# Order of the first planned steps, products of zeros on TensorE, and the planned length of u's load and product in an attention and feed-forward kernel

## The chip, the cores and the metric

The kernel runs on one core of a Trainium2 chip. The metric is the device time of one execution in microseconds (us). Eight runs of the kernel before gave 187.0, 188.34, 188.75, 187.57, 188.7, 187.79, 188.61 and 188.26 us: median 188.3 us.

The core has a matrix engine (TensorE, in the profile PE; PEld is its loading of the stationary operand), a vector engine (VectorE, DVE), an engine for activation functions (ScalarE, ACT), a general engine (GpSimd, POOL) and a queue (SyncE, SP) that issues nearly all transfers between main memory and the core's own memory. Each takes its instructions strictly in the order in which the program gives them. They wait for one another by semaphores.

## The reference

An attention with a decaying state (4 sequences, 8 heads, 768 steps, 48 numbers per head), and behind it a feed-forward layer without a gate:

```python
for t in range(S):
    kt, vt, rt, wt = (k[:, :, t].copy(), v[:, :, t].copy(), r[:, :, t].copy(), w[:, :, t].copy())
    cur = np.einsum('bhd,bhe->bhde', u[None] * kt, vt)
    y[:, :, t] = np.einsum('bhd,bhde->bhe', rt, state + cur)
    state = wt[:, :, :, None] * state + np.einsum('bhd,bhe->bhde', kt, vt)
...
x = np.ascontiguousarray(attn_out.transpose(0, 2, 1, 3)).reshape(B * S, H * D)   # 3072 x 384
h = x @ w_in                    # 384 x 2048
g = np.maximum(0.01 * h, h)
return (g @ w_out).astype(np.float32)    # 2048 x 384
```

## The kernel before

The 3072 rows are cut into 24 chunks of 128 rows, 6 per sequence. Every chunk goes through two parts.

The attention part (the scan): logarithm of w (L360, ACT), running sums of it by products with triangular matrices (L544 and L554, or L714 and L719, PE), exponentials of the sums (L370, ACT), products of r and k with them into a tile called rk (L300, DVE or POOL), transposes of rk (L418, PE, copied out at L295 or L297 into rkT), scores (L652 or L764, PE), a mask (L436, DVE), the products that make y in the bank yp (L669 and L677, or L794 and L799, PE), the sum with the bonus term of u (L467, DVE), and the transpose of y (L481, PE) whose copy is xT. The state is carried from chunk to chunk (products at L617 or L775, sums at L456). The first four chunks are done as two pairs by `pair` (64 rows of each of two interleaved halves), all others by `single`.

The feed-forward part: for each chunk four groups of 12 products xT by w_in (L837, "up", one group for each quarter of the 2048 columns, 512 columns of a bank hp), a leaky ReLU (L879, ACT) into g, and four groups of 4 products g by w_out (L898, "down", in the bank op). The chunk's result is copied to o and sent out (L915).

All inputs are 32-bit, and the weights are cast to 16 bits on the core (L295 on ACT, L297 on DVE and POOL) in halves: w_in comes in four loads (quarters 0 to 3, L319), w_out in four (L324), each of 768 KB. Tile in4 holds quarter 0 of w_in, in5 quarter 1, in6 quarter 2, in7 quarter 3; in8, in9, in10 and in0 hold the quarters of w_out. Before them the pairs' w, k, r and v are loaded (L493, 384 KB each).

Nothing is issued in the order of the source. Each operation is a `step` of a `Plan`, with an engine, a planned duration, its dependencies and a priority. `Plan.order` plays the steps through once, at build time: whenever an engine is free it takes the ready step with the smallest priority, and the order of the planned starts is the order in which the instructions are written into the engines' queues. So the planned durations and priorities decide the order alone; the chip does not know them. `EARLY` is a list of step numbers found by a search: a step in it gets a priority ahead of all others, by its place, and a letter behind the number gives the engine (a = ACT, v = DVE, p = POOL).

While TensorE has no step in the first 24 us of the plan (`WARM`), the last loop of the kernel writes products of a tile of zeros into the bank op1 (L933): as many as fit into the planned gap ahead of each PE step, at an assumed length each. `spread_u` (L495 to L507) loads u on ACT's queue, spreads it over the 128 partitions by a 32-bit product on PE (L504) and copies it to ub (L507).

Of the kernel before, what the change touches and what calls it, by code (L numbers as in the profile page):

```python
# [126 lines left out]
def kernel(  # L127
# [32 lines left out]
    CASTS = 21  # L160

    EARLY = """
        0 4 1 2 3 5 8 61 7 6 12 58 11 16 13 14 15 21 32 59 17 23 24 18 20p 19 22 28 9a 60 29 30 10a 33
        25 26 31v 40 27 117 64 34 65a 51 36 41a 44 52 63 114 46 42 126 62 45 35 67 66 120 43 71 123 37
        53 47 129 68 132 48 69 135 72 38 75p 49 70 76 74 77p 78 50 81 79 73 87v 54 82 39 118a 85 80 96v
        83 119p 138 86 55 84a 91 115 116 56 95 88v 57 713 128p 715 89 714 97 717 716 127p 98v 719 718 99
        140 122p 729 90v 720 100 121 730 102 723 124a 125p 101 721 724 92v 103 722 727 93 130a 170 104
        94 725 728 131v 105 107 726 106v 731 108 133a 737 109 733 738 134v 110 734 747 136 137p 139 745
        111 748 141 735 142 112 746 144 154v 261 732 113 736 145 172 174 752 147 749 159 149p 155v 171
        146 739 753 148 742 750 200 156 158 152 143a 157v 150 160 755 229 153 151 176 743 162 161 177  # L170
        186 231 756 763 165 265 764 164 230 191 178 758 187v 740 765 232 179 163 759 751 181p 180 202
        233 166 188 766 204 167 190 182 173 245 184 767 206 168 185v 183a 754 192 169v 768 193 741 207
        769 246 194 209 201 771 208 234v 757 770 247 216 262 772 760 210
    """
    blocks = [1] * NCH

# [53 lines left out]
    with tc.manual_schedule():  # L230
# [50 lines left out]
        plan = Plan()  # L281

        def step(eng, dur, fn, pri, reads=(), writes=(), deps=(), wire=None, rows=0, **alts):

            d = list(deps)
            for x in writes:
                d += x.old
            i = plan.add(eng, dur, fn, d, pri, wire, rows, {eng: dur, **alts} if alts else None)
            for x in (*reads, *writes):
                x.steps.append(i)  # L290
            return i
# [204 lines left out]
        def spread_u():  # L496
            u_row = step(
                "ACT", 0.5,
                lambda: nc.scalar.dma_start(out=ur[:], in_=u.rearrange("h d -> (h d)").unsqueeze(0)),
                -1, wire=0.05)  # L500
            up = pre_r.take()
            s_ub = step(
                "PE", 0.7,
                lambda: nc.tensor.matmul(up.t[:, 0:DM], lhsT=onef[:], rhs=ur[:], start=True, stop=True),  # L504
                -1, writes=[up], deps=[u_row])
            return step(
                "ACT", 0.5, lambda: nc.scalar.copy(out=ub[:], in_=up.t[:, 0:DM]), 0.05, reads=[up], deps=[s_ub])  # L507
# [6 lines left out]
        def pair(n):  # L514
# [19 lines left out]
            if n == 0:  # L534
                u_ld = spread_u()
# [155 lines left out]
        def single(n):  # L691
# [12 lines left out]
            if n == 0:  # L704
                u_ld = spread_u()
# [216 lines left out]
        for rank, word in enumerate(EARLY.split()):  # L922
            i = int(word.rstrip("avp"))
# [5 lines left out]
        at = 0.8  # L929
        for i in plan.order():  # L930
            if plan.eng[i] == "PE" and at < WARM:
                for _ in range(int((plan.start[i] - at) * 0.7 / 0.13)):
                    nc.tensor.matmul(  # L933
                        op_r.tiles[1][:, 0:256], lhsT=zeros[:, 0:128], rhs=zeros[:], start=True, stop=True)
                at = plan.start[i] + plan.dur[i]
            if plan.alts[i]:
                plan.fn[i](plan.eng[i])
            else:
                plan.fn[i]()
# [30 lines left out]
```

## Time and profile before

| | before |
|---|---|
| median of 8 runs | 188.3 us |
| the profiled execution | 187.0 us |
| its span, from first to last instruction | 185.3 us |
| PE busy | 177.3 us (96%) |
| DVE, ACT, POOL busy | 65%, 63%, 55% |
| products of zeros (L933) | 60, busy 10.5 us |
| products up (L837) | 1152, busy 78.0 us |
| products down (L898) | 384, busy 75.2 us |

Columns of a line of the page's part 5: line, engine, operation, output <- input with their shapes, count | busy us, mean ns of one | idle time of the engine just before, and what ended it. A row of the timeline gives the start, the length (until the end of the last of the merged instructions), and the same names; an idle time over 0.15 us stands in brackets with its releaser. The ends of products are modelled, since they are pipelined: what a group of products occupies is read from start to start. Such differences are used below: 0.65 us for 4 products down, 0.67 us for 12 products up.

The landing times of the loads that matter here, read from the releasers and the transfer records of the profiled execution: the pairs' eight loads at 4.5, 6.0, 7.5, 9.0, 10.5, 12.0, 13.5 and 14.9 us, the eight loads of weights at about 18.2, 20.2, 22.6, 24.5, 26.5, 28.6, 30.7 and 32.9 us.

### The profile page before, as it was taken

The page shows a single profiled execution, that of the slowest core. Times are in us where ns is not written, and L with a number is a line of the kernel's source. Part 1 is how long each engine was busy: PE and PEld are TensorE (multiplying, and loading weights), DVE is VectorE, ACT ScalarE, POOL GpSimd, SP SyncE. Part 2 cuts the span into 40 slices and gives each one's busy share as a digit, 9 for nine tenths or more (in the row PEclk, how much of TensorE's full clock was granted, in tenths as well). Part 3 has the DMA queues.
Part 4 walks back from the last instruction along what each step waited for, and adds up shares of the span by engine and source line. Part 5 has one row for each costly group of instructions (what it writes and reads, how often), then busy time and mean ns, then how long its engine had stood idle before and what let it go on. Part 6 is the DMA issues. An engine that isn't in the chain of part 4 may idle for free.

```text
span 185.3 us, 6316 instructions
## 1 busy us (share of the span) xinstructions
PE 177.3 (96%) x2608; PEld 139.3 (75%) x2608; DVE 120.5 (65%) x232; ACT 116.0 (63%) x254; POOL 101.1 (55%) x142
## 2 busy tenths in 40 slices
PE   7989889999999999999999999999999999999992
PEld 4658767877788788887877787778878778788671
DVE  2388776658777787987668786667656676725111
ACT  3776847589665797688677578645465564633330
POOL 7798571143875798878784474361874445620000
PEclk9999999999999999999999999999999999999999
DMA  6999999889599989897999797976999999581202
GB/s 150 261 262 370 382 377 324 165 175 211 135 233 199 187 169 207 176 203 158 161 229 170 153 209 144 201 172 151 219 132 216 159 233 131 128 126 42 67 0 85
DMA packets 116383, 34.62 MB, mean 187 GB/s; under 512 B 109697, under 2 KB 114818, under 8 KB 116354
## 3 DMA queue, kind: packets, MB, share of 16 engines
q1 hardware_dynamic: 116352, 34.22, 86.0%
q8 instruction: 20, 0.33, 0.8%
q14 instruction: 9, 0.07, 0.1%
q10 hardware_dynamic: 2, 0.00, 0.0%
HBM read 25.17 MB, written 4.72 MB: 161 GB/s over the span
## 4 chain that ended last, share of the span: by engine, by line
PE 81%; DMA 8%; SPq 6%; issue 1%; POOL 1%; DVE 1%
PE op L898 33%; PE hp L837 33%; DMA in<-in_moe_w_out_dram 5%; SPq L493 5%; PE se L764 3%; PE yp L799 2%; DMA xT<-y 2%; PE cp L714 2%; PE yp L775 2%; PE yp L794 1%; POOL w_out_b L297 1%; SPq L319 1%; PE so L418 1%; PE se L418 1%; PE yp L481 1%
## 5 line engine op out<-in xcount | busy, mean ns | idle before, releaser
L879 ACT ACTIVATE g<-hp 128x512 bf16<-128x512 f32 x96 | 57.2, 597 | 40.0 <-PE hp L837 38.3
L837 PE MATMUL hp<-xT,w_in_b 128*128 128x128 bf16 x1152 | 78.0, 219 | 0.6 <-DMA xT<-y 0.3
L898 PE MATMUL op<-w_out_b,g 128*128 128x384 bf16 x384 | 75.2, 326 | 0.9 <-POOL w_out_b L297 0.9
L837 PEld LDWEIGHTS <-w_in_b 128*128 128x128 bf16 x1152 | 68.4, 98 | 7.3 <-DMA xT<-y 0.7
L898 PEld LDWEIGHTS <-g 128*128 128x128 bf16 x384 | 33.5, 98 | 16.8 <-issue 1.0
L300 POOL TENSOR_TENSOR sb<-s,a 128x384 bf16<-128x384 f32 x17 | 14.4, 845 | 29.9 <-DVE s L456 14.3
L300 POOL TENSOR_TENSOR ru<-in,ub 128x384 f32<-128x384 f32 x22 | 22.6, 1028 | 7.7 <-DMA in<-in_r_dram 7.7
L300 POOL TENSOR_TENSOR vs<-in,dg 128x384 f32<-128x384 f32 x22 | 18.9, 859 | 8.4 <-DVE dg L393 8.1
L300 POOL TENSOR_TENSOR ru<-ru,in 128x384 f32<-128x384 f32 x20 | 20.8, 1041 | 0.9
L436 DVE TENSOR_TENSOR m<-se,maskb 128x512 bf16<-128x512 f32 x20 | 13.8, 688 | 11.2 <-PE so L764 8.0
L467 DVE TENSOR_TENSOR y<-yp,vs 128x384 bf16<-128x384 f32 x24 | 13.3, 554 | 10.2 <-PE yp L799 7.4
L300 DVE TENSOR_TENSOR rk<-in,ek 128x384 bf16<-128x384 f32 x18 | 13.5, 752 | 3.7 <-ACT ek L370 2.5
L370 ACT ACTIVATE cp<-cp 128x384 f32<-128x384 f32 x22 | 10.6, 482 | 6.3 <-DVE ci L729 6.3
L393 DVE TENSOR_REDUCE dg<-ru 128x8 f32<-128x384 f32 x24 | 13.1, 545 | 2.0 <-POOL ru L300 1.9
L360 ACT ACTIVATE lw<-in 128x384 bf16<-128x384 f32 x24 | 12.2, 520 | 3.5 <-DMA in<-in_w_dram 3.1
L729 DVE TENSOR_TENSOR ci<-cp,lw 128x384 f32<-128x384 f32 x20 | 11.0, 551 | 5.0 <-PE cp L719 3.3
L300 DVE TENSOR_TENSOR rk<-in,cp 128x384 bf16<-128x384 f32 x22 | 12.0, 547 | 2.5 <-ACT cp L370 1.9
L436 DVE TENSOR_TENSOR m<-so,maskb 128x512 bf16<-128x512 f32 x20 | 13.6, 680 | 0.0
L297 DVE COPY o<-op 128x384 f32<-128x384 f32 x10 | 5.6, 557 | 11.1 <-PE op L898 11.0
L933 PE MATMUL op<-zeros 128*128 128x256 bf16 x60 | 10.5, 303 | 1.1 <-DVE zeros L268 1.1
L370 ACT ACTIVATE ek<-ci 128x384 f32<-128x384 f32 x20 | 10.4, 519 | 0.8 <-POOL ru L300 0.7
L297 POOL CAST vb<-in 128x384 bf16<-128x384 f32 x19 | 10.2, 539 | 0.6 <-DMA in<-in_v_dram 0.6
(117 smaller groups left out, 210.9 us busy)
## 6 DMA issues: line engine op xcount, KB each, us to landing
out_dram<-o SPq DMA_DIRECT2D x24, 192.0 KB, 3.1
in<-in_w_dram SPq DMA_DIRECT2D x20, 192.0 KB, 4.1
in<-in_r_dram SPq DMA_DIRECT2D x20, 192.0 KB, 3.7
in<-in_k_dram SPq DMA_DIRECT2D x20, 192.0 KB, 3.7
in<-in_v_dram SPq DMA_DIRECT2D x20, 192.0 KB, 3.6
in<-in_moe_w_in_dram SPq DMA_DIRECT2D x4, 768.0 KB, 11.4
in<-in_moe_w_out_dram SPq DMA_DIRECT2D x4, 768.0 KB, 12.8
in<-in_w_dram SPq DMA_DIRECT2D x2, 384.0 KB, 4.9
```

The lines of the kernel that those rows point to most:

```text
L297: (nc.vector if e == "DVE" else nc.gpsimd).tensor_copy(out=o, in_=i)
L300: (nc.vector if e == "DVE" else nc.gpsimd).tensor_tensor(out=o, in0=a, in1=b, op=ALU.mult)
L360: lambda: nc.scalar.activation(out=lw.t[:, :, 0:D], in_=wn.t, func=AF.Ln),
L370: "ACT", 0.5, lambda: nc.scalar.activation(out=out.t[:], in_=i, func=AF.Exp, scale=scale),
L393: lambda: nc.vector.tensor_reduce(out=dg.t[:], in_=ru.t[:], axis=AX.X, op=ALU.add),
L436: lambda par=par: nc.vector.tensor_tensor(out=m.t[:, par], in0=gt(sc[par].t), in1=mask.unsqueeze(1).to_broadcast([128, NP, 128]), op=ALU.m ...
L467: lambda: nc.vector.tensor_tensor(out=y.t[:], in0=hd(yp.t[:, 0:DM]), in1=vs.t[:], op=ALU.add),
L729: lambda: nc.vector.tensor_tensor(out=ci.t[:], in0=hd(cp.t[:, 0:DM]), in1=lw.t[:, :, 0:D], op=ALU.add),
L837: nc.tensor.matmul(hp.t[:, a * N : (a + 1) * N], lhsT=w_in_b[:, t, (j + a) * 128 : (j + a + 1) * 128], rhs=xT[:, t, c0 : c0 + N], start=(a ...
L879: lambda hp=hp, g=g, j=j, J=J, N=N: nc.scalar.activation(out=g.t[:, j : j + J, 0:N], in_=hp.t[:, 0 : J * N].rearrange("p (a n) -> p a n", ...
L898: nc.tensor.matmul(op.t[:, 0:DM], lhsT=g.t[:, j, off : off + 128], rhs=w_out_b[:, j, :], start=(j == 0), stop=(j == NJ - 1))
L933: nc.tensor.matmul(op_r.tiles[1][:, 0:256], lhsT=zeros[:, 0:128], rhs=zeros[:], start=True, stop=True)
```

## The change

Three numbers in the code and the list `EARLY`. The list, cut to its first two lines:

```diff
     EARLY = """
-        0 4 1 2 3 5 8 61 7 6 12 58 11 16 13 14 15 21 32 59 17 23 24 18 20p 19 22 28 9a 60 29 30 10a 33
-        25 26 31v 40 27 117 64 34 65a 51 36 41a 44 52 63 114 46 42 126 62 45 35 67 66 120 43 71 123 37
...
+        0 4 1 2 3 5 8 58 7 6 11 60 12 14 13 16 20p 17 21 59 15 32 26 22 24 18 19 23 27 30 61 33 10v 25a
+        28 9v 29a 36 34 40 63 117 31v 62 35 41 44 66 45 42 114 67 120 51 68 71 87 126 43 69 123 76 72
...
@@ spread_u
                 lambda: nc.scalar.dma_start(out=ur[:], in_=u.rearrange("h d -> (h d)").unsqueeze(0)),
-                -1, wire=0.05)
+                -1, wire=0.75)
             up = pre_r.take()
             s_ub = step(
-                "PE", 0.7,
+                "PE", 1.6 / 1.8,
                 lambda: nc.tensor.matmul(up.t[:, 0:DM], lhsT=onef[:], rhs=ur[:], start=True, stop=True),
@@ the last loop
-                for _ in range(int((plan.start[i] - at) * 0.7 / 0.13)):
+                for _ in range(int((plan.start[i] - at) / 0.22)):
                     nc.tensor.matmul(
                         op_r.tiles[1][:, 0:256], lhsT=zeros[:, 0:128], rhs=zeros[:], start=True, stop=True)
-                at = plan.start[i] + plan.dur[i]
+                at = plan.start[i] + plan.dur[i] * (1.8 if plan.start[i] < 6 else 1)
```

The old list has 272 entries, the new one 339. `Plan.order` multiplies a planned PE duration by 1.8 when it starts before 6 us; the last loop now does the same when it counts the gap.

The steps and their dependencies are the same in both kernels; 34 steps of the first chunks change their engine. What the two built programs hold, read from their instruction streams:

Products of zeros: 60 before, 48 after. Ahead of u's product 12 and 13; between u's product and the first running sums 10 and 4 (and 1 before, none after, among the sums); ahead of the first transposes 6 and 5; the rest in ones to sevens up to the first product up.

The loads on SP, in order (pair 2 is chunks 2 and 3):

```
before: pair 0 w k r v | pair 2 v w k r | w_in 1, 0 | w_out 0 | w_in 2, 3       | w_out 1, 2, 3
after:  pair 0 w k r v | pair 2 w r k v | w_in 1, 0 | w_in 2  | w_out 0 | w_in 3 | w_out 1, 2, 3
```

Behind these the single chunks' loads (192 KB each) also change places among themselves.

PE, from the products that make y of chunk 0 on (z = products of zeros; up q c0 = group of 12 products up, quarter q, chunk 0):

```
before: y0 z5 turn-y0 z5 turns y1 turn z1 turn z6 turn-y1 state z1 | up0 c0, up0 c1, z1, up1 c0, up1 c1,
        down0 c0, scores, down0 c1, up2 c1, up2 c0, y2, up3 c1, up3 c0, turn-y2, scores, down1 c0, ...
after:  y0 z1 turns z3 turn-y0 z4 y1 state z2 turn-y1 z1 | up0 c0, up0 c1, z1, up1 c0, up1 c1,
        scores, up2 c0, up2 c1, down0 c0, down0 c1, y2, up3 c0, up3 c1, turn-y2, scores, down1 c1, ...
```

Here y0 is L669 with L677 of chunk 0, turn-y the transposes at L481, state the 16 products at L617 of pair 2, scores L652, y2 the products of chunk 2.

ACT, from about 16 us on:

```
before: xT0, pa, copy rkT, w_in 1 (half), copy rkT, copy rkT, w_in 0 (half), xT1, leaky ReLUs ...
after:  copy rkT, vb, copy rkT, pa, vb, w_in 1 (half), xT0, w_in 1 (other half), w_in 0 (half), xT1, leaky ReLUs ...
```

The other half of w_in 0 goes from DVE to POOL, one half of w_in 1 from POOL to ACT; the halves of w_out 0 are both on POOL before, one on DVE and one on POOL after; of w_out 1 one on ACT and one on DVE before, one on ACT and one on POOL after; of w_out 2 one on ACT in both, the other from DVE to POOL; of w_out 3 one on DVE and one on POOL before, both on DVE after. The shrunken states of pair 2 (L300, sb<-s,pa) go from DVE to POOL.

More of the change, by code (lines that the diff above doesn't have):

```diff
@@ L162 @@
     EARLY = """
-        0 4 1 2 3 5 8 61 7 6 12 58 11 16 13 14 15 21 32 59 17 23 24 18 20p 19 22 28 9a 60 29 30 10a 33
-        25 26 31v 40 27 117 64 34 65a 51 36 41a 44 52 63 114 46 42 126 62 45 35 67 66 120 43 71 123 37
-        53 47 129 68 132 48 69 135 72 38 75p 49 70 76 74 77p 78 50 81 79 73 87v 54 82 39 118a 85 80 96v
-        83 119p 138 86 55 84a 91 115 116 56 95 88v 57 713 128p 715 89 714 97 717 716 127p 98v 719 718 99
-        140 122p 729 90v 720 100 121 730 102 723 124a 125p 101 721 724 92v 103 722 727 93 130a 170 104
@@ L168 @@
[L168 to L172, printed above, removed]
@@ L173 @@
-        769 246 194 209 201 771 208 234v 757 770 247 216 262 772 760 210
+        0 4 1 2 3 5 8 58 7 6 11 60 12 14 13 16 20p 17 21 59 15 32 26 22 24 18 19 23 27 30 61 33 10v 25a
+        28 9v 29a 36 34 40 63 117 31v 62 35 41 44 66 45 42 114 67 120 51 68 71 87 126 43 69 123 76 72
+        75p 129 73 46 79 70 80a 77p 52 132 81 47 65a 78 37 82 53 83 74 85 64a 48 96 135 118a 86v 49 38
+        50 84 39 119 54 91v 95 115p 116 138 55 97 56 713 57 92v 98 715 93 714 122p 121 717 716 99 94 719
+        718 88v 100 127p 141 720 721 128v 723 722 101 729 724 102 730 125p 124a 89 103 90v 725 104 727
@@ new lines @@
+        130p 131 172 105 107 726 106v 732 108 728 733 109 133a 134p 737 734 731 738 735 136 139 747 110
+        137v 748 140 745 142 111 739 170 143v 746 144 112 740 736 145 171 186 113 742 147 751 158 229
+        149 146 752 743 159 148 154 231 152 162 753 749 160v 155 174 741 758 165 200 750 150 153v 176
+        759 187 201 755 156 151a 177 763 157 202 233 188 161 191 764 179 163 230 245 178 754 164 190 756
+        757 181p 192v 166 173 204 765 180 184 167 206 744 182 185 766 207 262 183 168 208 760 216 261
@@ L174 @@
+        169v 767 193 210 209 771 217 768 194 761 235 769 772 195 211p 762 175a 212 218 232 775 770 189
+        236 196 213 776 214 203 246 773 197 237 779 215 239 263 198 774 247 220 264 782 265 222 199 785
+        223 238 241 248 293 777 249 234v 250 240 267 780 778 205 294 242 219 243 221 268 781 783 295 224
+        244 277 786 784 296 225 251 252 787 226 788
     """
```

## The prediction

> **What bounds the kernel now.** First the page's parts 1 and 4 (busy times, and the chain of work that ended last):
>
> ```profile
> PE 177.3 (96%) x2608; PEld 139.3 (75%) x2608; DVE 120.5 (65%) x232; ACT 116.0 (63%) x254; POOL 101.1 (55%) x142
> PE 81%; DMA 8%; SPq 6%; issue 1%; POOL 1%; DVE 1%
> ```
>
> TensorE is 81% of the chain; the transfers and their queue, 14%, can only be at the start. So second the chain in order of time, around the place where it goes over to PE:
>
> ```profile
> 11.70 0.74 SPq L319
> 12.49 10.10 DMA in<-in_moe_w_out_dram
> 22.64 2.28 POOL w_out_b L297 x2
> 24.96 0.81 PE op L898 x4
> ```
>
> Up to 22.6 us a load of w_out sets the pace, then its two casts one behind the other on POOL, and from 24.96 us PE never waits long. Third, what PE waited for in the first 45 us, and its timeline there:
>
> ```profile
> PE op L898 <- POOL w_out_b L297: 0.9, 1, 0.9
> PE op L544 <- ACT lw L360: 0.7, 1, 0.7
> PE se L652 <- issue: 0.3, 1, 0.3
> PE hp L837 <- DVE w_in_b L297: 0.3, 1, 0.3
> ```
>
> ```profile
> 21.05 1.51 PE L837 MATMUL hp<-xT,w_in_b 128*128 128x128 bf16 x24 [0.28 <-DVE w_in_b L297]
> 22.40 0.27 PE L933 MATMUL op<-zeros 128*128 128x256 bf16 x1
> 22.58 1.50 PE L837 MATMUL hp<-xT,w_in_b 128*128 128x128 bf16 x24
> 24.96 0.81 PE L898 MATMUL op<-w_out_b,g 128*128 128x384 bf16 x4 [0.89 <-POOL w_out_b L297]
> 26.08 0.82 PE L898 MATMUL op<-w_out_b,g 128*128 128x384 bf16 x4
> 26.74 1.50 PE L837 MATMUL hp<-xT,w_in_b 128*128 128x128 bf16 x24
> 28.18 0.36 PE L669 MATMUL yp<-sb,rkT 128*64 128x96 bf16 x8
> ```
>
> After 25 us PE loses 0.34 us at 31 us and 0.35 us near the end, where the last chunk's xT lands; all else is products that both kernels hold. So the change is worth what it takes out of PE's time up to its dense stretch: I compare the moment at which PE starts y2 (L669 of chunk 2, 28.18 us before), because both kernels have by then done the same products: up quarters 0 to 2 and down quarter 0 for two chunks, one group of scores.
>
> **What stands between 21.05 and 28.18 before.** Six groups up at 0.67 (two take 1.34 in the chain), two down at 0.65, scores 0.38 (25.70 to 26.08): 4.02 + 1.30 + 0.38 = 5.70 us. The other 1.4 us of 7.13 are 0.19 at 22.4 (a zero, and the wait for bank hp), 1.04 from 23.92 (22.58 + 1.34) to 24.96 (the wait for POOL's casts of w_out), 0.09 and 0.10 of seams.
>
> **The change, first up product.** In the new ACT queue the copy xT0 stands behind the cast of w_in quarter 1, which cannot start before its load has landed:
>
> ```profile
> 16.34 0.48 ACT L295 COPY xT<-yp 128x384 bf16<-128x384 bf16 x1
> 18.19 0.83 ACT L295 CAST w_in_b<-in 128x768 bf16<-128x768 f32 x1 [0.36 <-DMA in<-in_moe_w_in_dram]
> 20.22 0.83 ACT L295 CAST w_in_b<-in 128x768 bf16<-128x768 f32 x1 [0.23 <-DMA in<-in_moe_w_in_dram]
> ```
>
> Behind xT0 waits bank yp, for it y1 on PE, and behind y1 all of PE. Step by step: cast from 18.19; the next ACT instruction starts 0.1 before its end (18.93, as the trace has it), xT0 takes 0.48 to 19.41; y1 at 19.47 with 0.91 (y2 took 28.18 to 29.09), to 20.38; the sum y1 on DVE starts 0.18 later (as 29.09 to 29.27 did) and takes 0.56, to 21.12; the transposes at 21.18 with 0.17; one zero 0.11; first up product at 21.46. State products (0.45) and two zeros lie under the DVE sum. The other condition: w_in 0 lands at 20.2, its half on POOL takes between 0.83 and 1.15 us (POOL's casts of w_in), DVE's took 0.77: 21.1 to 21.4. So the start is 21.46 against 21.05, 0.4 later. Bounds: 21.1, if only the fastest cast counted, and 21.9, if POOL's half took as long as DVE's two casts at 32.94 together (1.67 us, from 20.2).
>
> **The change, behind it.** The third load of weights is now w_in 2, and the groups up2 stand ahead of down0. So: 21.46 + 5.70 + 0.19 for hp + 0.2 for seams = 27.55 for y2, against 28.18: 0.63 earlier. That is the 1.04 no longer waited, less the 0.41 of the later start. It holds if nothing else is late; landing (by its place among the loads), longest cast, and need:
> - scores at 24.3: DVE's last state sum stands behind the cast of w_in 2 (landing 22.6, 0.98 at most) and takes 0.56: 24.2. The tightest.
> - up2 at 24.7: DVE 23.6, POOL behind one sb (0.83 from 21.65) 23.8.
> - down0 at 26.1: 24.5, POOL 1.19: 25.7; DVE's half beside it.
> - up3 at 28.5: 26.5, on ACT behind the leaky ReLU of up2: 27.7.
> - down1 at 30.3: 28.6 + 1.19 = 29.8. Down2 and down3 at 33 and 36: 31.9 and, two casts by DVE in turn at 32.94 with 1.67, 34.6.
> A late hand-over costs what it is late: 0.1 to 0.4 us each. Later order, singles' loads included: PE did not wait over 0.15 us from 31 to 168 us before; I take nothing, bounds 0.3 either way (its waits of 0.28 and 0.34 are the nearest rows).
>
> **Edits I cost at nothing.** Zeros ahead of u: 13 at 0.213 from 1.12 end at 3.89, u's product takes 0.85 (3.79 to 4.64), four zeros at 0.109, 5.18; then the sums wait for the second logarithm (5.44), while before ten zeros held them to 5.74. So the scan starts 0.25 us earlier. Hidden behind the landing of w_in 1 at 18.2; without that cover it would be the same 0.25 gained. v of pair 2 lands 4.4 us later (14.9 for 10.5), w 1.5 earlier (10.5 for 12.0): v is needed by the state products at 20.4, covered by the wait for xT0.
>
> The pause of 0.34 at 31 us lies inside scores (start to start 0.53 lost) and no releaser is shown. The same scores follow the same groups in the new order, so I keep it; bounds: 0.53 gained, or 0.53 lost once more.
>
> **Sum.** 187.0 - 0.6 = 186.4 us on the profiled execution. That one is the fastest of the eight, 1.3 below the median; the 0.6 is taken off the median: 188.3 - 0.6 = 187.7 us. What a measurement can tell from no change is some 0.5%, 0.9 us.
>
> **Rivals.**
>
> *The array goes slow in the longer idle time (the slower side).* What the zeros do is seen in these rows:
>
> ```profile
> 1.12 2.74 PE L933 MATMUL op<-zeros 128*128 128x256 bf16 x12 [1.12 <-DVE zeros L268]
> 4.64 1.27 PE L933 MATMUL op<-zeros 128*128 128x256 bf16 x10
> ```
>
> and in the busy times of the stretch from 1 to 4 us (by engine; then granted clock, DMA share, GB/s):
>
> ```profile
> 1.00:4.00 3.00, 2.88 (x13) 1.85 (x14) 1.16 (x13) 1.08 (x1) 2.41 (x12) 1.00 0.70 171
> ```
>
> The same product comes every 0.213 us at first and every 0.109 us (1.10 for ten) from 4.64 on, after 3.5 us of work, though the granted clock (1.00) shows nothing. Before, PE then never idles over 0.73 us. In the new order turn-y0 (15.82 before) has up to four groups of transposes (0.22) and some zeros more ahead, so about 16 to 17.3; with its 0.17 and four zeros PE is empty from 16.6 to 17.9, until y1 at 19.47: 1.6 to 2.9 us idle. If that makes it slow again, the next 3.5 us of work take up to twice as long: 1.75 to 3.5 us, on the path. Then 188.3 - 0.6 + 1.75 to 3.5 = 189.4 to 191.2, say 190. It decides from 1.5 us of loss on. Against it: 0.73 of idle cost nothing; no row shows 2 us.
> [...]
>
> *The gain is eaten.* Scores 0.1 to 0.3 late, down0 0.2 late, a second pause of 0.3: 0.6 gone. The margins of 0.1 to 0.5 speak for it, that they are taken with the longest casts against. 188.1 to 188.6, say 188.3; this is also what comes out if the new order does not remove the wait.
>
> *More than forecast.* The pause falls elsewhere (0.53 gained), or y1 comes 0.35 sooner: 188.3 - 0.6 - 0.5 = 187.2, at best 186.9.
>
> **Numbers.** Forecast 0.45, more 0.20, eaten 0.18, slow array 0.17. Faster by over 0.5% (below 187.4): all of "more" and 0.2 of the forecast's 0.45, whose own range is 187.3 to 188.1 with the medians' scatter of a few tenths: 0.40. Slower (above 189.2): the slow array and 0.03 of the eaten: 0.20. Same: 0.40. Range: 186.6 (more, with scatter of 0.3) to 189.5 (the near end of the slow array).
>
> **What would show it.** In the new profile: first L837 near 21.4 and not 21.05; no wait of L898 for w_out near 25; y2 of chunk 2 near 27.5; an idle time of about 2 us before y1, released by the ACT copy of xT; products of y1 and up at 0.67 a group, not 1.3, and 48 products of zeros. Wrong it is if up groups behind that idle time take over 1 us, if L652 or L898 between 24 and 36 us wait for DVE or POOL, or if waits over 0.3 us appear on PE after 36 us.

## The result, and the profile after

| | before | after |
|---|---|---|
| median | 188.31 us (59 runs, 186.3 to 189.29) | 189.29 us (22 runs, 187.71 to 189.74) |
| profiled execution, its span | 187.0, 185.3 us | 189.97, 188.3 us |
| first product up (L837, now L840) | 21.05 us | 21.89 us |
| y2 (L669, now L672) | 28.18 us | 29.08 us |

The ratio is 1.0047, 95% interval 1.003 to 1.0065: slower by half a per cent, where 0.3% faster was forecast. (The ratios in this text leave out runs more than 1.5% above the fastest of their kernel; among the experiments below that is five of twelve in a_oldzeros and three of twelve in a_pause and in a_oz66, so there the ratio lies below that of the medians.) All lines of the new source stand three further down. The new page, parts 1 and 4:

```profile
PE 178.6 (95%) x2596; PEld 138.8 (74%) x2596; DVE 122.0 (65%) x230; ACT 116.7 (62%) x254; POOL 105.4 (56%) x144
PE 85%; DMA 5%; ACT 3%; issue 2%; DVE 2%; SPq 0%; DVEq 0%; ACTq 0%
```

The shares of transfers and of SP's queue have fallen from 14% to 5%, and TensorE has nearly the same work. What is left of them in the chain is late: 4.87 us of a load of w at 146 us and 4.07 of the last transposition of y at 174. (Before, that transposition was in the chain too, with 3.57 us at 171, so not all of the 14% lay at the start, as the prediction has it.) "Issue", time with no releaser in the profile, has doubled. The main waits of PE in the first 40 us, behind its first product:

```profile
PE op L620 <- DVE vb L300: 1.0, 1, 1.0
PE so L655 <- issue: 0.9, 1, 0.9
PE se L655 <- issue: 0.6, 1, 0.6
PE yp L672 <- ACT xT L298: 0.4, 1, 0.4
```

The wait for w_out's casts is gone. In its place stand 0.9 and 0.6 us inside scores. PE's timeline shows where:

```profile
21.89 1.50 PE L840 MATMUL hp<-xT,w_in_b 128*128 128x128 bf16 x24
23.41 1.50 PE L840 MATMUL hp<-xT,w_in_b 128*128 128x128 bf16 x24
24.84 0.21 PE L655 MATMUL se<-rkT 48*64 48x64 bf16 x1
...
26.12 0.21 PE L655 MATMUL so<-rkT,rkT 48*64 48x64 bf16 x1 [0.91 <-issue]
26.34 1.51 PE L840 MATMUL hp<-xT,w_in_b 128*128 128x128 bf16 x24
27.69 1.46 PE L901 MATMUL op<-w_out_b,g 128*128 128x384 bf16 x8
29.08 0.36 PE L672 MATMUL yp<-sb,rkT 128*64 128x96 bf16 x8
...
32.59 0.21 PE L655 MATMUL se<-rkT,rkT 48*64 48x64 bf16 x1 [0.65 <-issue]
```

The first scores take 1.50 us (24.84 to 26.34) and not 0.38. The groups up keep 0.67 us each and L901 follows at once. Late in the run, from 140 to 182 us, there are two more waits; before, there was one, of 0.3:

```profile
PE hp L840 <- DMA xT<-y: 0.9, 1, 0.9
PE cp L717 <- ACT lw L363: 0.7, 1, 0.7
```

Set against the first profile of before, work for work: 0.90 us later at y2, 0.3 more at the second scores, 0.9 more near 150 us, 0.5 more near 176 us, and 0.3 in small ones. The medians differ by only 1.0, because that first profile of before is one of its short executions; another one of the same program (before_again, below) took 189.41 us. The 0.90 us at y2 stands against both: y2 starts at 28.18 us in each.

### The profile page after: what moved, and what is told of

Same layout as the page of the kernel before. It is cut to its first block, busy times and chain, and to the rows that moved or that the text cites. A ratio compares the mean times of both kernels' runs of the same rounds, so it can differ in the third digit from the quotient of the medians.

```text
span 188.3 us, 6289 instructions
## 1 busy us (share of the span) xinstructions
PE 178.6 (95%) x2596; PEld 138.8 (74%) x2596; DVE 122.0 (65%) x230; ACT 116.7 (62%) x254; POOL 105.4 (56%) x144
## 4 chain that ended last, share of the span: by engine, by line
PE 85%; DMA 5%; ACT 3%; issue 2%; DVE 2%; SPq 0%; DVEq 0%; ACTq 0%
PE hp L840 32%; PE op L901 31%; PE se L767 3%; DMA in<-in_w_dram 3%; PE op L936 3%; DMA xT<-y 2%; PE yp L802 2%; PE cp L717 2%; PE yp L778 2%; PE yp L797 1%; PE yp L484 1%; PE so L421 1%; PE yp L680 1%; PE se L421 1%; DVE vb L300 1%
## 5 line engine op out<-in xcount | busy, mean ns | idle before, releaser
L840 PE MATMUL hp<-xT,w_in_b 128*128 128x128 bf16 x1152 | 77.5, 219 | 0.9 <-DMA xT<-y 0.9
L901 PE MATMUL op<-w_out_b,g 128*128 128x384 bf16 x384 | 75.0, 326 | 0.0
L840 PEld LDWEIGHTS <-w_in_b 128*128 128x128 bf16 x1152 | 68.5, 98 | 7.5 <-DMA xT<-y 1.2
L901 PEld LDWEIGHTS <-g 128*128 128x128 bf16 x384 | 33.3, 97 | 15.8
L303 POOL TENSOR_TENSOR ru<-in,ub 128x384 f32<-128x384 f32 x23 | 24.8, 1078 | 17.5 <-DMA in<-in_r_dram 17.1
L303 POOL TENSOR_TENSOR vs<-in,dg 128x384 f32<-128x384 f32 x23 | 19.5, 848 | 13.9 <-DVE dg L396 13.7
L303 POOL TENSOR_TENSOR ru<-ru,in 128x384 f32<-128x384 f32 x22 | 23.2, 1055 | 1.1
L303 POOL TENSOR_TENSOR sb<-s,a 128x384 bf16<-128x384 f32 x15 | 13.1, 877 | 17.3 <-DVE s L459 11.1
L300 DVE COPY o<-op 128x384 f32<-128x384 f32 x10 | 5.6, 558 | 16.5 <-PE op L901 16.4
L303 DVE TENSOR_TENSOR rk<-in,ek 128x384 bf16<-128x384 f32 x18 | 14.4, 799 | 0.9 <-ACT ek L373 0.7
L300 POOL CAST vb<-in 128x384 bf16<-128x384 f32 x17 | 8.6, 503 | 4.4 <-DMA in<-in_v_dram 4.4
L936 PE MATMUL op<-zeros 128*128 128x256 bf16 x48 | 9.8, 338 | 1.1 <-DVE zeros L271 1.1
```

What stands on the lines that cost most here:

```text
L300: (nc.vector if e == "DVE" else nc.gpsimd).tensor_copy(out=o, in_=i)
L303: (nc.vector if e == "DVE" else nc.gpsimd).tensor_tensor(out=o, in0=a, in1=b, op=ALU.mult)
L840: nc.tensor.matmul(hp.t[:, a * N : (a + 1) * N], lhsT=w_in_b[:, t, (j + a) * 128 : (j + a + 1) * 128], rhs=xT[:, t, c0 : c0 + N], start=(a ...
L901: nc.tensor.matmul(op.t[:, 0:DM], lhsT=g.t[:, j, off : off + 128], rhs=w_out_b[:, j, :], start=(j == 0), stop=(j == NJ - 1))
L936: nc.tensor.matmul(op_r.tiles[1][:, 0:256], lhsT=zeros[:, 0:128], rhs=zeros[:], start=True, stop=True)
```

## The experiments

**A pattern in the traces.** I numbered PE's instructions (loads of the stationary operand, products and the few of its sequencer together, by their start, from 0; a load can start ahead of the product before it, as 369 loads of the changed kernel do, by up to 0.05 us, so a number is good to a few places). In the changed kernel PE stands still between instructions 704 and 705 and between 960 and 961; before, between 960 and 961. 961 - 705 = 256. The trace has 20 transfers of the kind "instruction" on queue 8, 16,384 bytes each, and 5,199 instructions of PE: 260 to a transfer on average, near the 256 between the two places. In the changed kernel two of them run from 23.48 to 24.53 and from 30.01 to 31.12 us; PE goes on at 26.12 and 32.59, 1.6 and 1.5 us behind their ends. Theory: PE stands at each 256th instruction when the instruction transfer that goes with it is late, and the time is set by where in the program such an instruction falls. Rivals: the fewer zeros, with which the array's full rate comes later (9.48 us against 3.84 in the first trace of before); the new order itself; chance.

All runs, with their traces; a_ is made from the changed kernel, b_ from the kernel before. "Full rate" is the first entry of full rate in the trace's record of the granted clock; the pauses are named by instruction number (0.2 us and more, in the first 60 us); "last xT" is the time from issue to landing of the last transposition of y (L473, now L476), and "loss" what PE lost behind it. Each ratio is to runs of the kernel before taken beside that run; their medians were 187.89 to 188.38 us, so medians of different rows compare to about half a microsecond only.

```
run           median (range, n)             ratio to before [95%]    full rate  up0    pauses at: us                      last xT  loss
before        188.31 (186.3-189.29, 59)                               3.84      21.05  961: 0.53                          3.57     0.51
before_again  188.50 (186.94-189.41, 12)    1.0009 [0.9974, 1.0043]   8.21      22.11  449: 0.49, 961: 1.30               4.00     0.94
after         189.29 (187.71-189.74, 22)    1.0047 [1.003, 1.0065]    9.48      21.89  449: 0.38, 705: 1.10, 961: 0.84    4.07     1.02
after_again   188.86 (187.94-190.04, 12)    1.0051 [1.002, 1.0081]    8.85      21.89  449: 0.37, 705: 1.08, 961: 0.84    4.03     0.98
a_oldzeros    188.02 (185.82-188.94, 12)    0.9942 [0.9896, 0.9988]   5.12      21.60  449: 0.57, 961: 0.62               3.03     0
a_idx26       187.55 (185.41-187.77, 12)    0.9945 [0.9911, 0.998]   11.76      22.80  449: 1.09, 961: 0.83               3.11     0.06
a_shift66     186.34 (185.89-187.6, 12)     0.9908 [0.9879, 0.9936]  10.48      21.89  961: 0.48                          2.32     0
a_oz66        187.86 (185.56-189.45, 12)    0.9938 [0.9899, 0.9976]  10.04      23.42  961: 0.75                          2.32     0
a_pause       188.54 (186.58-189.64, 12)    0.9993 [0.996, 1.0025]    9.52      24.55  449: 1.55                          2.33     0
a_shift256    190.38 (188.63-191.55, 6)     1.0112 [1.0056, 1.0168]   9.92      22.68  705: 0.23, 961: 1.28, 1217: 0.84   3.72     0.66
a_late36      188.51 (188.34-189.31, 12)    1.0043 [1.0023, 1.0062]   8.51      21.89  449: 0.34, 705: 1.06, 961: 0.84    2.81     0
b_newzeros    186.43 (186.02-186.68, 6)     0.9898 [0.9851, 0.9945]   9.57      21.70  961: 0.58                          2.32     0
b_idx26       187.10 (186.08-187.84, 12)    0.9945 [0.992, 0.9969]    7.83      21.71  961: 0.61                          3.77     0.72
b_shift148    186.49 (185.97-188.16, 12)    0.9937 [0.9909, 0.9966]   8.42      22.86  none                               2.33     0
b_nz148       187.17 (186.27-187.93, 12)    0.9957 [0.9923, 0.999]   10.96      22.34  1217: 0.23                         2.33     0
b_late36      187.98 (186.61-188.4, 12)     0.9991 [0.9965, 1.0018]   9.22      22.35  449: 0.29, 961: 1.31               2.39     0
```

**One part alone.** before_again is the kernel before, unchanged. a_oldzeros is the changed kernel with the old formula for zeros (13 more of them), b_newzeros the kernel before with the new one (13 fewer):

```diff
-                for _ in range(int((plan.start[i] - at) / 0.22)):
+                for _ in range(int((plan.start[i] - at) * 0.7 / 0.13)):
...
-                at = plan.start[i] + plan.dur[i] * (1.8 if plan.start[i] < 6 else 1)
+                at = plan.start[i] + plan.dur[i]
```

> The kernel before, unchanged, for a second profile and for what no change looks like. Both theories: ratio 1.00 within 0.002, about 188.3 us; in the profile TensorE pauses after its 961st instruction, inside scores (L652), by about 0.5 us.

> The changed kernel with the old count of products of zeros (13 more, all other instructions in the same order). Theory Z (the fewer zeros leave the array at half rate until 8.4 us, and that makes the first up product 0.4 us late): zeros 0.109 us apart from about 4.6 us, first up product at 21.4 to 21.5, time 0.4 us below the changed kernel, 188.9. Theory F (TensorE stands still at fixed instruction counts until its next instructions have come): both pauses inside scores stay, since the count moves by 26 only, so no more than that is gained. Rival (the zeros are the whole loss): 188.3 or less. Rival (the zeros do nothing): 189.3.

> The kernel before with the new count of products of zeros alone (same order of all else). Theory Z: array at half rate until about 8.4 us, but the first up product waits for the landing of w_in 0 at 20.2 all the same: 188.3 to 188.6. Rival (the zeros are the whole loss): 189.3.

Both formulas gained when put into the other kernel, so the number of zeros can't be what decides by itself. Each zero is two instructions: both edits also move all that follows by 26 places. That b_newzeros was the faster by 1.0% was a miss of mine. So was a_oldzeros in part: both pauses were to stay, and that at 705 went (its 128 instructions ahead took 3.81 us there, not 2.85).

**Positions alone.** a_shift66 cuts the changed kernel's first 13 zeros into 46 smaller ones of about the same array time: 66 more instructions ahead, nothing else moved.

```diff
-                for _ in range(int((plan.start[i] - at) / 0.22)):
+                n, nc_, nr = (46, 72, 64) if at == 0.8 else (int((plan.start[i] - at) / 0.22), 256, 128)
+                for _ in range(n):
                     nc.tensor.matmul(
-                        op_r.tiles[1][:, 0:256], lhsT=zeros[:, 0:128], rhs=zeros[:], start=True, stop=True)
+                        op_r.tiles[1][0:nr, 0:nc_], lhsT=zeros[:, 0:nr], rhs=zeros[:, 0:nc_], start=True, stop=True)
```

> The changed kernel with its 13 leading products of zeros (256 columns, 128 rows) cut into 46 (72 columns, 64 rows): as much streaming, but every later instruction of TensorE stands 66 places further on. Theory F: the pauses after instruction 705 and 961 now fall among products up, which take long enough, and are gone: scores take 0.4 us each from start to start instead of 1.5 and 1.2, and 1.0 to 1.9 us come off the changed kernel's time: 187.4 to 188.3. Rival (the pauses belong to the scores' products, or to what they wait for): they stay, 189.3.

0.9% below the kernel before and, by the ratios, 1.4% below the changed one; that is more than I expected (187.4 to 188.3 us), though a pause of 0.48 us at 961 stayed. Up to the first scores its trace is the changed kernel's to 0.02 us; then, PE's timeline:

```profile
23.41 1.50 PE L840 MATMUL hp<-xT,w_in_b 128*128 128x128 bf16 x24
25.22 1.51 PE L840 MATMUL hp<-xT,w_in_b 128*128 128x128 bf16 x24
26.57 1.46 PE L901 MATMUL op<-w_out_b,g 128*128 128x384 bf16 x8
27.96 0.36 PE L672 MATMUL yp<-sb,rkT 128*64 128x96 bf16 x8
```

The third row comes 1.12 us sooner than its twin above: scores take 0.38 again. Instruction 705 is now a product up, reached at 24.02, 2.0 us behind the end of its transfer.

The same cut with other numbers gives the next five: a_idx26 is (26, 128, 64), 26 places, those of a_oldzeros; b_idx26 is b_newzeros with (23, 112, 64), back at the places of before; b_shift148 is before with (86, 36, 32); a_shift256 cuts all 48 zeros into 176, 256 places, one whole step of the pattern; b_nz148 is b_newzeros with all zeros cut, 148 places from before.

> The changed kernel with the first 13 products of zeros cut into 26 of half the columns: 26 more TensorE instructions (13 loads, 13 products) ahead of all that follows, the same array time, nothing else moved. It has the instruction positions that the changed kernel with the old formula for zeros had, and the changed kernel's late full rate. Theory (pauses at TensorE instructions 705 and 961 of the stream): instruction 705 now lies 26 program steps earlier, ahead of the first scores of the second pair, so the pause of 1.1 us there goes; one of about 0.6 us stays at 961; 186.5 to 188.2 us. Rival (too few zeros, array at half rate until 8.4 to 9.5 us): nothing of that is mended, 189.0 to 189.5 us.

> The kernel before with the new formula for zeros, and the first 10 of its zeros cut into 23 of 111 columns, so that every later instruction stands again at the position of the kernel before. If the gain of the new formula alone (186.43 against 188.38 us) came from the moved positions, this run is back at 188.0 to 188.6 us; if it came from the zeros themselves, it stays at 186.2 to 186.8 us.

> The kernel before with its first 12 products of zeros cut into 86 of 36 columns and 32 rows: 148 more TensorE instructions ahead of all that follows, nothing else moved. Theory (pauses at fixed positions of the stream): the pause of 0.53 us inside the second scores goes and none takes its place; the span falls by 0.4 to 0.6 us and the median to 186.5 to 187.9 us. Rival (the positions mean nothing): 188.2 to 188.6 us, and the pause stays inside the same scores.

> The changed kernel with its 48 zeros cut into 176 smaller ones of about the same array time: 256 more instructions, one whole step of the positions, so that the same products as in the changed kernel stand at the places where TensorE pauses. Theory (position modulo 256): nothing is gained; pauses of 0.8 to 1.3 us inside the same two groups of scores, the last transposition of y meets an instruction transfer again and takes 3.5 to 4.2 us; 188.4 to 189.8 us. Rival (small zeros, or more instructions ahead, help by themselves, as 66 more seemed to): 186.0 to 187.0 us.

> The kernel before with the new formula for zeros, and the zeros cut so that the stream stands 148 instructions later than in the kernel before: the positions of the run without any pause (186.49 us), with the 13 zeros of 0.11 to 0.21 us less. If the two gains add up: no pause at 705, 961 and 1217, the last transposition of y at 2.3 us, and 185.6 to 186.3 us, below both kernels by over 1%. If fewer zeros give nothing on top: 186.3 to 186.8 us.

a_idx26: the pause at 705 is gone as expected, 1.7 us off the median, though one of 1.09 at 449 came, which I had not expected; its ratio of 0.9945 beside the 0.9942 of a_oldzeros, at the same places, shows nothing gained by 13 more zeros. b_shift148: no pause, as expected. a_shift256 is the test that could have sunk the theory: with 256 more instructions the pauses stand in the same two groups of scores, at 961 and 1217:

```profile
27.27 0.21 PE L655 MATMUL so<-rkT,rkT 48*64 48x64 bf16 x1 [1.09 <-issue]
```

and it is 1.1% slower than before: neither small zeros nor more of them help. (It is 1.1 us above the changed kernel; its cut zeros fill 0.8 us more up to the first product up.) b_idx26 fell between its two cases: both the zeros and their places may have had a part in b_newzeros, but the intervals of the two runs overlap (0.9851 to 0.9945 and 0.992 to 0.9969), so this is not shown. b_nz148 missed: without a pause above 0.23, its median was 187.17. Its trace has the full rate only at 10.96 us and the first product up 1.3 us later than the first trace of before; the two gains did not add up, and I did not separate why.

In all 29 pauses of 0.15 us or more that lie at a number 193 + 256 k in the first 40 us of these traces, PE went on 1.3 to 1.6 us behind the end of the transfer. Nor did PE come to any of these numbers from 449 on sooner than 1.3 us behind it where there was no pause. What that time behind the end consists of, the traces do not show.

**A delay of known cause; the array's rate.** a_pause is a_shift66 with 36 instead of 46 small zeros ahead and ten full zeros in front of the first scores of pair 2 (1.1 us). a_oz66 is a_oldzeros at the places of a_shift66, (35, 110, 64).

```diff
+            if i == 100:
+                for _ in range(10):
+                    nc.tensor.matmul(
+                        op_r.tiles[1][:, 0:256], lhsT=zeros[:, 0:128], rhs=zeros[:], start=True, stop=True)
```

> The changed kernel with 66 more instructions ahead as in the run that took the pauses out (186.34 us), but ten products of zeros of 0.109 us put in front of the first scores of the second pair: 1.1 us lost at the place where the changed kernel pauses, by a cause that is known. If only the pause itself is lost: 187.2 to 187.6 us. If the waits near 150 and 176 us of the changed kernel's trace follow from such a delay: 188.2 to 189.4 us, with those waits in its trace.

> The changed kernel with the old formula for zeros (13 more of them) and its first 15 zeros cut into 35 of 110 columns, so that the stream stands 66 instructions later than in the changed kernel, as in the run that reached 186.34 us. If zeros matter by the time at which the full rate is granted (5.12 us in the trace with the old formula, 9.48 us in the changed kernel's), the first up product starts up to 0.7 us earlier and the median falls to 185.5 to 186.2 us. If the positions are all, 186.1 to 186.7 us.

a_pause: PE was 1.8 us behind the changed kernel at 100 us, yet without a wait near 150 or 176 us: in this trace, of the longest of its twelve executions (189.64 us), those waits did not follow from being late. It is confounded in one point: with 20 places fewer ahead of y0 than a_shift66, instruction 449 fell into y0 and cost 1.55 us. Its row in PE's timeline, and behind it the windows (stretch, length, PE busy and count, granted clock, DMA share, GB/s):

```profile
19.25 0.24 PE L680 MATMUL yp<-vb,m 64*64 64x48 bf16 x4 [1.36 <-issue]
```

```profile
16.00:20.00 4.00, 2.52 (x54) 0.97 1.05 386
20.00:23.00 3.00, 3.00 (x34) 0.50 1.07 379
23.00:26.00 3.00, 3.00 (x73) 0.97 1.05 378
```

Behind the pause the granted clock was at half from 19.76 to 23.18 us (0.50 in the second window). a_oz66 missed both its cases. It has runs from 185.56 to 189.45 us; in its trace the full rate came at 10.04 us, and with its 13 further zeros, nine of them 0.21 us apart ahead of the first running sum, that sum starts at 7.93 us (6.41 in the changed kernel) and the first product up 1.5 us behind a_shift66's. More zeros did not make the rate come early here, and with a late rate they cost.

**The changed kernel again, and the late transfers alone.** a_late36 and b_late36 are the two kernels with 18 tiny zeros in front of the first product down of chunk 12, so that only what lies behind 112 us is moved, by 36 instructions:

```diff
                 def down(op=op, g=g, q=q, off=off, ch=ch):
+                    for _ in range(18 if ch == 12 and q == 0 else 0):
+                        nc.tensor.matmul(
+                            op.t[0:16, 0:16], lhsT=zeros[:, 0:16], rhs=zeros[:, 0:16], start=True, stop=True)
```

> The changed kernel once more, for a second trace. Theory: TensorE stands again at instructions 705 and 961, 0.8 to 1.3 us each, and goes on 1.35 to 1.65 us after the end of the instruction transfer; the moment of the full rate differs, since it came at 3.84 and at 8.21 us in two traces of the kernel before. The waits near 150 and 176 us may be there or not. Median 188.6 to 189.5 us. Rival: the two pauses were chance, and this trace has neither.

> The changed kernel with 18 tiny products of zeros (16 by 16) in front of the first product down of chunk 12, near 100 us: 36 instructions more behind that place alone, nothing moved before it; they cost TensorE some 0.4 to 0.9 us there (18 at the 0.03 to 0.05 us at which the smallest zeros followed one another). Theory: the pauses at 705 and 961 stay as they are (1.1 and 0.8 us), but the last instruction transfers run 1 us earlier against the data: the one that met the last transposition of y 1.6 us after its issue now starts 0.5 to 0.7 us after it, the transposition takes 3.0 to 3.2 us instead of 4.0, and the wait near 176 us is gone. Median 188.2 to 189.2 us. Rival (that wait comes from loads that are late, not from the instruction transfer): transposition at 3.6 to 4.1 us and the wait of 0.8 to 1.0 us stay, 189.3 to 190.2 us.

> The same 18 products in the kernel before. Theory: the pause at 961 stays (0.5 to 1.3 us), the last transposition of y takes 2.3 to 3.2 us instead of 3.6 to 4.0, its wait of 0.5 to 0.9 us goes; with the 0.4 to 0.9 us of the products 187.6 to 188.6 us. Rival: the wait stays and the products come on top, 188.7 to 189.4 us.

after_again repeats the changed kernel's first 100 us to 0.02 us, both pauses included; the wait near 176 us is there, that near 150 is not. In both late runs the early pauses stayed and the wait near 176 us went. The transfers in the trace's window from the issue of the last transposition (queue 8 is the instruction transfer), first the changed kernel, then a_shift66, then a_late36:

```profile
q8 instruction: 1, 0.02, 2.0%
...
xT<-y SPq DMA_TRANSPOSE x1, 4.1
```

```profile
xT<-y SPq DMA_TRANSPOSE x1, 2.3
```

```profile
q8 instruction: 1, 0.02, 1.9%
...
xT<-y SPq DMA_TRANSPOSE x1, 2.8
```

Over all 16 traces: where an instruction transfer starts 1.0 to 1.7 us behind the issue, the transposition takes 3.6 to 4.1 us and PE loses 0.5 to 1.0 us (six traces); where it starts 0.1 to 0.6 behind, 2.8 to 3.1 us and at most 0.06 (three); otherwise 2.3 to 2.4 and nothing (seven). a_late36 also draws the runs together, eleven of twelve lie within 188.34 to 188.75; less the 0.6 its products cost, that is 187.9 us, the changed kernel's shortest runs. By the ratios (1.0043 with these products, 1.0047 without) the gain is 0.7 us and not 1.4.

## Why the prediction was wrong

**The failed step: "The same scores follow the same groups in the new order, so I keep it; bounds: 0.53 gained, or 0.53 lost once more."** I tied the pause to the scores, kept it at 0.53, and put a second one at nothing in the sum. The step is right for the second scores alone; ahead of the first scores a group down is gone in the new order. In these traces the pauses belong to every 256th instruction, and a price would have needed the time of the 128 or so instructions ahead: in the pauses of 0.2 us and more the transfer started 0.2 to 2.0 us after the instruction 128 places ahead, took 1.0 to 1.1 us, and PE went on 1.3 to 1.6 us later. Before, instruction 705 also stands in the first scores, but the 128 ahead of it took 5.5 us, the wait of 1.04 and a group down among them; its transfer was over at 21.50 and PE came at 25.73. In the new order they take 2.85 us: transfer over at 24.53, PE there at 25.01, on at 26.12. The wait for w_out is not what covered it: in before_again, without that wait, the 128 take 3.99 us, and PE comes 1.63 us behind the end of the transfer and doesn't pause. There, as in the first trace, a group down and 10 of the scores' small instructions are among the 128; in the new order there are no group down and 42 of them. a_shift66 takes the pause away and a_shift256 brings it back. The old pause at 961 stayed too, and grew from 0.53 to 0.84 (1.30 in before_again).

**First product up: the mechanism right, the term too small.** 0.41 later was forecast, 0.84 was measured against the first trace of before. ACT's rows:

```profile
18.52 0.83 ACT L298 CAST w_in_b<-in 128x768 bf16<-128x768 f32 x1
19.37 0.48 ACT L298 COPY xT<-yp 128x384 bf16<-128x384 bf16 x1
```

"Cast from 18.19" began at 18.52, because ACT came to it late, and xT0 stood 0.85 behind it, not 0.74. ACT was late because the scan was: "u's product takes 0.85", "four zeros at 0.109" and "the scan starts 0.25 us earlier" took full rate from about 4 us for granted. After:

```profile
4.01 1.64 PE L507 MATMUL op<-ur,onef 1*128 1x384 f32 x2
5.58 1.03 PE L936 MATMUL op<-zeros 128*128 128x256 bf16 x4
6.41 0.53 PE L547 MATMUL cp<-lw,pex 128*128 128x384 bf16 x1
```

u takes 1.57 us, the four zeros 0.83, and the first running sum starts at 6.41 (5.74 before). The full rate came at 9.48. With the same order and the rate at 5.12 (a_oldzeros) the cast starts at 18.22 and the first product up at 21.60: 0.29 of the missing 0.43 may be the rate; that trace also has 13 more zeros and a pause of 0.57 ahead of y1, so the share is not shown. The new planned length of u, 1.6 us, is what the product took where the full rate came late (1.57 us here), against 0.85 in the first trace of before; and 3.84 us is the exception among three traces that start as before does (8.21 in before_again, 9.22 in b_late36). PE's timeline of before_again:

```profile
3.79 1.64 PE L504 MATMUL op<-ur,onef 1*128 1x384 f32 x2
```

There u takes 1.58 us too (its next row starts at 5.37).

**The wait that was to be saved.** "That is the 1.04 no longer waited, less the 0.41 of the later start" reads one trace of before. In before_again the first product up came later than in the changed kernel, and PE did not wait for w_out at all:

```profile
22.11 1.50 PE L837 MATMUL hp<-xT,w_in_b 128*128 128x128 bf16 x24
24.97 0.81 PE L898 MATMUL op<-w_out_b,g 128*128 128x384 bf16 x4
28.18 0.36 PE L669 MATMUL yp<-sb,rkT 128*64 128x96 bf16 x8
```

In b_late36 it was so too (22.35, y2 at 28.42). From the first product up to y2 it is 6.07 us in before_again, b_late36, a_shift66 and a_oz66 alike, 7.13 with the wait (the first trace of before) and 7.19 with the pause (the changed kernel). So the wait for w_out was what an early start ran into, in one of three traces; it took nothing from the later ones.

**What was right.** y2 of before at 28.18 as the mark to compare with; no wait for w_out, down0 and up2 on time, no wait of the scores for DVE (the margins held), groups up at 0.67, 48 zeros, 5.70 us of work to y2. With the two terms put right from the trace the sum meets it, so the rest of the sum held: 27.55 forecast for y2, plus 0.43, plus 1.10, is 29.08; and a_shift66, without the pause, has 27.96, 0.22 earlier than before. So this order's own gain at y2 was 0.2 and not 0.63. With the big pauses out of both, the two orders stand at 186.34 (a_shift66) and 186.49 us (b_shift148), ratios 0.9908 and 0.9937, with intervals that overlap.

**"Later order ... I take nothing, bounds 0.3 either way"** failed too: 1.02 us near 176 (0.51 before), and 0.89 near 150 in one of two traces. The first stands behind a transposition that takes 4.07 us, with an instruction transfer 1.6 us behind its issue: a_late36 moves what lies behind 112 us alone, and there the transposition takes 2.81 us and the loss is 0 (2.39 and 0 in b_late36). In the second a load of w, from 146.21 to 151.08 us, meets an instruction transfer as well (147.64 to 149.49), but this was not tried alone and stays open. Between the changed kernel and a_shift66 lie 2.95 us by the medians, 2.6 by the ratios. The pauses are 1.5 of it (1.12, and 0.84 less the 0.48 that a_shift66 still has), the late waits 1.4 by the medians of a_late36 and 0.7 by the ratios; up to 0.4 us stay open.

**The rivals.** "The array goes slow" did not come: PE's idle time ahead of y1 was 0.36 us, not 1.6 to 2.9, since turn-y0 came only at 18.77, and the full rate held from 9.48 on. But a_pause shows the half rate at this very place, for 3.42 us, behind a pause of 1.55 us, with PE busy for 2.52 of the 4.00 us up to 20. So there, in one trace, it came behind a pause near the lower end of the forecast idle time; how long an idle time has to be was not tried, and the 1.75 to 3.5 us were my estimate from the distances of zeros before, 0.213 and 0.109 us. "The gain is eaten" came nearest in kind, with "a second pause"; 0.3 was too small a price for it, and the array's rate and the late transfer came on top. The median was set against the profile rightly (0.6 off the median, not off 187.0), but one trace of before hid that its own losses behind y2 range from 1.0 (0.53 and 0.51) to 3.4 us (before_again: 1.30, then 1.15 in three waits from 134 to 158 us, then 0.94).

**Open.** Why 13 zeros fewer help the old order at equal places (b_idx26, 0.9945); why b_nz148 does not add the gains up; the wait near 150 us.

## What to carry to other kernels

Before pricing a new order, number the instructions of the busiest engine, find in a trace where its pauses lie, and see whether they keep a step (here 256, at 193 + 256 k, and here in the first 35 us alone). Where the 128 ahead of such a place were small and dense (scores, here 64 instructions in 0.38 us), the pause was 0.84 to 1.10 us in the changed kernel, and cutting a few idle-time products moved it for nothing (a_shift66 against the changed kernel: 186.34 for 189.29 us). An edit that added or dropped instructions early was therefore here never only that edit (13 zeros more or fewer moved all that follows by 26 places); compare it at equal positions. A wait that a change is to remove may cover a late start, so see if it stands in other executions too. And take two or three traces of the kernel before: how soon the array runs at full rate differed by 4.4 us between two executions of one program.

## What the runs showed of the hardware

- PE paused at its instructions 193 + 256 k, by 0.2 to 1.55 us, in the first 35 us, and went on there 1.3 to 1.6 us behind the end of an instruction transfer (16,384 bytes, 0.9 to 2.0 us each). From 40 us on, in the traces of before and after, 256 instructions took 7.9 to 11.3 us, PE came to each of these numbers 5.6 us or more behind the end of its transfer (the transfers counted in order, the first with 449), and no idle time stands there.
- The last transposition took 3.6 to 4.1 us where an instruction transfer started 1.0 to 1.7 us behind its issue (six traces), 2.8 to 3.1 where it started 0.1 to 0.6 us behind (three), and 2.3 to 2.4 otherwise (seven). With 36 instructions more from 112 us on, 4.07 became 2.81 us (a_late36).
- The full rate came at 3.84 to 11.76 us in 16 traces, in before at 3.84 and at 8.21. The spread was 8 us over all kernels and 4.4 within one. Why it mostly came so late was not tried; the product of u, with one row of operand and 1.57 us long in the changed kernel, stands in that time.
- Once granted, the rate was lost again for 3.42 us behind a pause of 1.55 us (a_pause, one trace). Pauses of up to 1.31 us in the other traces had no such end.
